# Every engine of a gated-memory kernel in a written order, with eight PSUM banks in turn and TensorE turning part of q and k

## The chip, the cores and the metric

One core of a Trainium2 chip. The metric is the device time of one execution in microseconds (us), of which several are taken; the span given with a profile runs from the first to the last instruction of one profiled execution.

## The reference

Four batches (B), eight heads (H), 768 tokens (S), 40 numbers a head (D), so 320 a token over all heads. First a recurrent attention with exponential gates, then a gated block with a causal convolution of five taps:

```python
def _attn_ref(q, k, v, i_gate, f_gate, o_gate):
    for t in range(S):
        m_new = np.maximum(f_gate[:, :, t] + m, i_gate[:, :, t])
        f_stab = np.exp(f_gate[:, :, t] + m - m_new)
        i_stab = np.exp(i_gate[:, :, t] - m_new)
        C = f_stab[:, :, None, None] * C + i_stab[:, :, None, None] * np.einsum('bhd,bhe->bhde', vt, kt)
        n = f_stab[:, :, None] * n + i_stab[:, :, None] * kt
        denom = np.maximum(np.abs(np.einsum('bhd,bhd->bh', n, qt)), 1.0)
        y[:, :, t] = sigmoid(o_gate) * np.einsum('bhde,bhe->bhd', C, qt) / denom
def _moe_ref(x, w_val, conv_w, w_out):
    gate_pre = sum(conv_w[k] * xp[:, k:k + S, :] for k in range(5))
    return (1.0 / (1.0 + np.exp(-gate_pre)) * (x @ w_val)) @ w_out
```

(`vt`, `kt`, `qt` are token t of v, k and q; `xp` is x with four zero rows ahead.) The second part's x is y with the heads side by side. Its weights arrive as float64 and are turned into float32 on the chip by integer operations (lines 586 to 606).

## The kernel before

The 768 tokens are six tiles j of 128. A tile and a batch b make a unit u, so there are 24; each unit has two chunks of 64 tokens, 48 chunks g in all. The recurrence over time is written per chunk as products of matrices, with the running state C and n carried from a chunk of a batch to the next.

*Preparation, per tile and batch.* q and k are loaded (L188, L192), the largest magnitude is taken on ScalarE (`prep_max`, L288), a power of two as scale comes from it on VectorE (`prep_scale`, L293 to L300), and each number becomes two float16 parts: the high part in `prep_hi` (L324 GpSimd for tile 0, L326 ScalarE for q, L327 VectorE for k of the later tiles), the low one in `prep_lo` (L332 VectorE). They lie in `stk`, tokens on partitions. `prep_tr` (L350) turns a half, q or k of one batch, with a DMA that transposes, issued on SP's queue, into `tq` or `tk`: 48 such transfers. k is also copied into `kp` by DMAs (L197), v and the output gate are loaded (L201, L204).

*Per chunk.* `args` (L360, TensorE) forms sums of gates into `psd`, `expo` (L371, ScalarE) their exponential `dm`. `scores` (L387, TensorE, eight products) gives q times k, `pss`; `probs` (L394, VectorE) multiplies scores by decays into `pt`. `keyw` (L406) weights the keys on GpSimd, `state` (L421, TensorE) makes the next state in `pc`, `state_out` (L434, ScalarE) copies it out. `heads` (L444, TensorE) reads the result out into `ph`.

*Per unit.* `norm` (L459 to L463, VectorE) forms one over the denominator, `norm_o` (L468, GpSimd) multiplies the output gate by it, `gate_o` (L473, VectorE) gives x. `x_tr` (L482) turns x on TensorE in three pieces, `x_copy` (L490 to L492, ScalarE) copies it out of PSUM, once rounded for TensorE and once whole; `x_rest` takes the low part (L498, GpSimd), the piece of 64 channels (L497, VectorE) and the four last tokens of the tile before (L500, L501, GpSimd).

*Per tile, the gated block.* `conv0` (L507, GpSimd) is the first tap, `conv` (L513, VectorE) the others, eight per tile; `conv3` (L525, TensorE) the last 64 channels as ten products; `sigmoid` (L533). `val` (L548, TensorE, three groups of eight products into `pf`), `z_mul` (L553, VectorE), `z_hi` (L557, ScalarE) and `z_lo` (L562, GpSimd) split the product into two parts, `outp` (L574, TensorE, eight products into `po`), `outp_st` (L579, ScalarE) and `out_dma` (L583). The last tile does this in halves of two batches.

*The order.* The start is written out by hand (L692). The rest gets a due time from the table `LAGS`, in units of a chunk; all steps are sorted by it into a program:

```python
    ctx.enter_context(tc.manual_schedule(engines={mybir.EngineType.SP}))
    ps_s = ctx.enter_context(tc.tile_pool(name="ps_s", bufs=NSH, space=PS))
    ps_h = ctx.enter_context(tc.tile_pool(name="ps_h", bufs=2, space=PS))
    ps_c = ctx.enter_context(tc.tile_pool(name="ps_c", bufs=1, space=PS))
    for _, _, fn, a in sorted(work, key=lambda w: w[:2]):
        fn(*a)
```

SP's queue runs in this program order; the other engines get theirs from the framework's scheduler, which starts from it and may move instructions. PSUM has eight banks: five (`ps_s`) serve all short work, two (`ps_h`) `heads`, one (`ps_c`) `state`.

Of the kernel before, what the change touches and what calls it, by code (L numbers as in the profile page):

```python
# [18 lines left out]

LAGS = {  # L20
    "cons1": -5.183, "cons1d": 0, "cons2": 0.457, "cons2d": 2.675, "wgt": 3.44, "wgtd": 0.804, "close": 2.831,
    "og": -7.359, "kp": -5.611, "kpd": 1.009, "vc": -3.927, "vcd": 0.989, "nat": -14.361, "natd": 0.826,
    "sig_o": -3.584, "max": -9.51, "hi": -8.451, "lo": -6.85, "lod": 0.308, "tr": -5.254, "den": -0.323,
    "dend": 0.177, "rs": 1.457, "gate": 3.86, "x_tr": 4.721, "x_copy": 6.057, "x_rest": 7.056, "args": -3.401,
    "expo": -3.399, "scores": -2.076, "probs": -1.445, "keyw": -2.703, "state": -0.531, "state_out": 0.189,
    "heads": -0.632, "conv0": 4.698, "conv0d": 0.9, "conv": 5.393, "convd": 0.299, "sig": 8.436, "val": 8.878,
    "vald": 0.463, "z": 9.375, "zh": 9.181, "zl": 9.511, "outp": 13.042, "outpd": 0.257, "ob": 15.39, "od": 14.45,
    "sig0": -0.329, "maxd": 0.014, "early": 0.441, "conv3": 8.55, "scaled": 0, "e_conv0": 5.797, "e_conv0d": 0.226,
    "e_conv": 4.49, "e_convd": 0, "e_conv3": 3.873, "e_sig": 7.715, "e_val": 6.616, "e_vald": 0.359, "e_z": 8.556,
    "e_zh": 8.123, "e_zl": 8.811, "e_outp": 11.131, "e_outpd": 0.989, "e_ob": 9.909, "e_od": 11.211, "half": 2.582,  # L30
    "si1": 1.548, "og1": 4.264, "sig1": 4.352, "vc1": -3.33, "kpe": 0, "natq": -13.409, "natqd": 0, "qmax": -10.547,
    "qmaxd": 0.075, "qhi": -9.634, "qlo": -8.762, "qtr": -8.036, "qd": 1.073, "qmul": -9.356, "qout": -3.776,
    "kpi": 6.531, "qe1": 0.864, "nat2": 0.089, "og2": -0.141, "sig2": -0.871, "qe2": 0.725, "og3": -0.415,
    "tr3": 0.74, "kp0": -1.411, "si1q": 1, "on_act_hi": 0, "on_act_dup": 0, "on_dve_state": 0, "on_dve_out": 0,
    "on_dve_x": 0, "on_dve_xl": 0, "on_dve_rs": 0, "on_dve_kw": 0, "on_dve_zl": 0, "z@2": 13.103, "zh@2": 13.406,
# [907 lines left out]
```

## Time and profile before

| | |
|---|---|
| median of 3 runs | 287.59 us (287.15 to 287.76) |
| profiled execution, own time | 289.57 us |
| its span | 287.8 us |
| mean granted clock of TensorE | 0.905 |
| busy: TensorE, VectorE, ScalarE, GpSimd | 228.3, 223.5, 172.6, 156.1 us |

The profiled execution is one of its own, 1.98 us over the median. Busy time counts instructions that work; register, branch, semaphore and DMA-issuing ones are left out. PE is TensorE, PEld its loading of weights (which lies beside PE), DVE VectorE, ACT ScalarE, POOL GpSimd and SP SyncE. Matmuls are pipelined and their ends are modelled, so a busy PE is not one at its peak.

### The profile page before, as it was taken

Reading aid. Unit: us, or ns where it says so; the run is one execution under the profiler, and the core shown is the slowest. Engines: PE = TensorE matmul, PEld = TensorE weight load, DVE = VectorE, ACT = ScalarE, POOL = GpSimd, SP = SyncE. Lnnn points to the kernel's source line nnn. Section 1 sums busy time; section 2 is a strip of 40 time slices with the busy share of each in tenths; the row PEclk is TensorE's granted clock in tenths of the full one; section 3 lists DMA queues with packets and bytes.
Section 4 is the critical chain, followed back from the end, with each engine's and each line's share of the span. In section 5 each row is a group of like instructions: output and inputs, shape, how many; then the busy total and the mean of one; then the engine's idle time right before and its main releaser. Section 6 shows DMA issues by size and latency. Waiting matters only on the chain.

```text
span 287.8 us, 6601 instructions
## 1 busy us (share of the span) xinstructions
PE 228.3 (79%) x2411; PEld 186.9 (65%) x2411; DVE 223.5 (78%) x498; ACT 172.6 (60%) x376; POOL 156.1 (54%) x236
## 2 busy tenths in 40 slices
PE   0038827835976876977899999989999999999885
PEld 0027626624865765655698776876678977887874
DVE  7899979746799999877998679997359944973940
ACT  4266555574797774589664596853595466346262
POOL 7694614322878465848935349541369162944451
PEclk9999999575895579999589999996899999999999
DMA  7899899998999996999963899949759640020112
GB/s 139 150 143 176 113 204 142 202 199 135 203 164 224 186 170 62 186 172 208 171 64 59 148 217 208 158 61 167 181 129 128 168 62 3 0 71 24 46 48 92
DMA packets 145897, 38.73 MB, mean 135 GB/s; under 512 B 135176, under 2 KB 143752, under 8 KB 145864
## 3 DMA queue, kind: packets, MB, share of 16 engines
q1 hardware_dynamic: 143044, 37.76, 83.6%
q10 hardware_dynamic: 2820, 0.54, 1.2%
q8 instruction: 19, 0.31, 0.5%
q14 instruction: 14, 0.11, 0.2%
HBM read 17.87 MB, written 4.23 MB: 77 GB/s over the span
## 4 chain that ended last, share of the span: by engine, by line
PE 45%; DMA 16%; DVE 9%; SPq 4%; issue 4%; ACT 3%; POOL 3%; ACTq 0%; DVEq 0%; POOLq 0%
PE ph L444 12%; PE po L574 7%; PE pss L387 6%; DMA tk<-stk 6%; PE pc L421 5%; PE pf L548 5%; PE pg L525 4%; PE psd L360 3%; DMA kp<-nat 3%; PE px L482 3%; DVE sg L513 3%; DMA vc<-in_v_dram 3%; SPq L350 2%; DMA nat<-in_q_dram 2%; DVE pt L394 2%
## 5 line engine op out<-in xcount | busy, mean ns | idle before, releaser
L444 PEld LDWEIGHTS ph<-vc,pt 128*64 128x64 f32 (+1 forms) x768 | 57.6, 159 | 24.4 <-ACT vc L434 12.0
L444 PE MATMUL ph<-vc,pt 128*64 128x41 f32 (+1 forms) x768 | 63.5, 251 | 11.5 <-ACT vc L434 9.1
L406 POOL TENSOR_TENSOR kw<-kp,dm 128x320 f32<-128x320 f32 (+1 forms) x44 | 36.9, 841 | 31.1 <-PE pc L421 12.0
L421 PE MATMUL pc<-vc,kw 128*40 128x41 f32 (+1 forms) x704 | 43.8, 225 | 11.8 <-POOL kw L406 7.3
L513 DVE SCALAR_TENSOR_TENSOR sg<-xc,cwt,sg 128x512 f32<-128x512 f32 (+1 forms) x56 | 48.0, 884 | 3.2 <-POOL sg L507 3.1
L421 PEld LDWEIGHTS pc<-vc,kw 128*40 128x40 f32 (+1 forms) x704 | 37.5, 138 | 18.6 <-issue 9.1
L394 DVE SCALAR_TENSOR_TENSOR pt<-pss,cmp,dm 128x512 f32<-128x512 f32 x48 | 35.5, 741 | 10.1 <-PE pss L387 6.5
L387 PE MATMUL pss<-tq,tk 120*128 120x64 f16 x384 | 33.4, 259 | 8.1 <-DMA tk<-stk 3.4
L360 PE MATMUL psd<-ra,la 120*128 120x512 bf16 x48 | 22.8, 475 | 20.5 <-DMA la<-gda 18.6
L468 POOL TENSOR_TENSOR rs<-sg,den 128x320 f32<-128x320 f32 x24 | 20.5, 854 | 32.1 <-DVE den L463 23.8
L371 ACT ACTIVATE dm<-psd 128x512 f32<-128x512 f32 x48 | 28.4, 596 | 13.6 <-issue 6.5
L387 PEld LDWEIGHTS <-tk 120*128 120x128 f16 x384 | 26.4, 128 | 14.9 <-issue 7.2
L332 DVE SCALAR_TENSOR_TENSOR stk<-nat,scl,stk 128x320 f16<-128x320 f32 x48 | 31.4, 662 | 4.0 <-ACT stk L326 3.3
L288 ACT ACTIVATE junk<-nat 128x320 bf16<-128x320 f32 x48 | 22.5, 469 | 17.0 <-DMA nat<-in_q_dram 7.5
L498 POOL TENSOR_TENSOR xl<-xc,xh 128x256 fp32r<-128x256 f32 x24 | 20.0, 833 | 22.8 <-ACT xc L491 22.8
L434 ACT COPY vc<-pc 40x328 f32<-40x328 f32 x44 | 18.7, 425 | 15.8 <-PE pc L421 14.3
L553 DVE TENSOR_TENSOR sg<-pf,sg 128x512 f32<-128x512 f32 (+3 forms) x21 | 12.6, 610 | 13.5 <-ACT sg L533 6.9
L326 ACT ACTIVATE stk<-nat,scl 128x640 f16<-128x640 f32 x20 | 16.1, 822 | 9.9 <-DMA tq<-stk 7.3
L562 POOL TENSOR_TENSOR zl<-sg,zh 128x512 fp32r<-128x512 f32 (+1 forms) x14 | 15.9, 1139 | 11.0 <-ACT zh L557 10.9
L574 PE MATMUL po<-woh,zh 128*128 128x320 f32 x72 | 20.2, 337 | 0.8 <-POOL zh L562 0.8
L360 PEld LDWEIGHTS <-la 120*128 120x128 bf16 x48 | 5.7, 120 | 20.5 <-issue 19.5
L574 PE MATMUL po<-wol,zh 128*128 128x320 f32 x72 | 18.4, 309 | 0.0
(151 smaller groups left out, 465.9 us busy)
## 6 DMA issues: line engine op xcount, KB each, us to landing
nat<-in_q_dram SPq DMA_DIRECT2D x24, 160.0 KB, 3.4
vc<-in_v_dram SPq DMA_DIRECT2D x12, 320.0 KB, 5.6
sg<-in_o_gate_dram SPq DMA_DIRECT2D x6, 640.0 KB, 7.3
out_dram<-ob SPq DMA_DIRECT2D x24, 160.0 KB, 1.9
kp<-nat SPq DMA_DIRECT2D x22, 160.0 KB, 4.3
nat<-in_k_dram SPq DMA_DIRECT2D x10, 320.0 KB, 4.1
...
```

What stands on the lines that cost most here:

```text
L288: nc.scalar.activation(junk, part(j, x, i), AF.Abs, accum_out=amx[j % 2][:, x, i : i + 1])
L332: return nc.vector.scalar_tensor_tensor(t[:, :, lo : lo + D], part(j, x, i), scl[j % 2][:, x, i : i + 1], t[:, :, 0:D], op0=ALU.mult, op1= ...
L360: nc.tensor.matmul(psd, la[:, p, j, b], ra[:, :, j], start=True, stop=True,)
L371: nc.scalar.activation(dm, psd_[g], AF.Exp)
L387: nc.tensor.matmul(o, tk[h], tq[:, h], start=True, stop=True)
L394: nc.vector.scalar_tensor_tensor(pt, pss_[g], cmp_[j % 2][:, p, b : b + 1], dmt[g], op0=ALU.mult, op1=ALU.mult)
L406: (nc.vector if turn("on_dve_kw", b) else nc.gpsimd).tensor_mul(kw[0:n], kp[0:n, p, b * H : (b + 1) * H], dmt[g][0:n, :, L - 1 : L].to_bro ...
L421: nc.tensor.matmul(pc[n0 : n0 + D, h], kwt[g][0 : ROWS[p], h], vc[j % 2][0 : ROWS[p], p, b * H + h], start=True, stop=True)
L444: nc.tensor.matmul(pht[u][p * L : (p + 1) * L, h], ptt[g][0 : ROWS[p], h], vc[j % 2][0 : ROWS[p], p, b * H + h], start=True, stop=True,)
L468: (nc.vector if turn("on_dve_rs", b) else nc.gpsimd).tensor_mul(rs, og[j % 2][:, b * H : (b + 1) * H], dnt[u].to_broadcast([P, H, D]))
L513: nc.vector.scalar_tensor_tensor(o, xc[j % 2][:, c, b0:b1, t : t + P], cwt[:, c, t : t + 1], o, op0=ALU.mult, op1=ALU.add)
L574: nc.tensor.matmul(pf, z, w, start=(i == 0), stop=(i == len(mm) - 1))
```

## The change

The table of due times and the sort are gone. A string `PLAN` lists every step of the program; a step names its function, its numbers and the engine (`=V` VectorE, `=A` ScalarE, `=P` GpSimd, `=S` SP) or, for TensorE, the PSUM bank (`#0` to `#7`). All engines now run in that written order. The eight banks are one set; any step takes any bank. Buffers are picked by the chunk's or unit's number.

```diff
-    ctx.enter_context(tc.manual_schedule(engines={mybir.EngineType.SP}))
+    ctx.enter_context(tc.manual_schedule())
...
-    ps_s = ctx.enter_context(tc.tile_pool(name="ps_s", bufs=NSH, space=PS))
-    ps_h = ctx.enter_context(tc.tile_pool(name="ps_h", bufs=2, space=PS))
-    ps_c = ctx.enter_context(tc.tile_pool(name="ps_c", bufs=1, space=PS))
+    banks = [psp.tile([P, 512], F32, name=f"bank{i}") for i in range(8)]
...
+ldq.2.3=S wcv.5.7=V laj.1=V args.2#1 trp.0.3.0#3 scs.1.1.2.0.2.1=V lo.0.3.1=V ldk.2.0.2=S expo.0=A wcv.0.0=V ldv.0.1=S
...
+    def trp(b, j, i, x):
+        t = banks[b].bitcast(F16).rearrange("p (h n) -> p h n", h=H)
+        for h in range(H):
+            nc.tensor.transpose(t[0:K3, h], stk[(j * B + i) % NSTK][:, x, h, 0:K3], id16)
+        late["tr", j, i, x] = t
+
+    def trc(e, j, i, x):
+        put[e](turned(j, i, x)[0:K3], late["tr", j, i, x][0:K3])
...
+    for step in PLAN.split():
+        step, _, b_ = step.partition("#")
+        step, _, e = step.partition("=")
+        name, *num = step.split(".")
+        steps[name](int(b_) if b_ else e, *(int(n) if n.isdigit() else n for n in num))
```

What else differs:

- *Turning.* `trp` turns a half of tiles 0 and 1 with eight TensorE transposes into a bank read as float16, `trc` copies it to `tq` or `tk`: 16 halves, 7 copies on VectorE and 9 on ScalarE. `trd` is the DMA for tiles 2 to 5: 32 transfers instead of 48.
- *Engines.* Weighted keys: 24 GpSimd and 20 VectorE (44 GpSimd before). Output-gate product: 17 and 7 (24 and 0). Low part of x: 10 and 14 (24 and 0). Low part of z: 2 and 19 (21 and 0). The low parts of the weights: 7 on VectorE. High parts of q and k: 37 ScalarE, 8 VectorE, 3 GpSimd (20, 20 and 8). Of the copies out of PSUM that ScalarE made, VectorE takes 10 of the state, 6 of the output, 6, 5 and 6 of the three of x; and 6 of the 21 roundings of z. The carried tokens of x go to all three engines (GpSimd before).
- *The spread of the gate sums* (`spread_out`, L258 and L263) is issued on SP's queue, one piece excepted (ScalarE's before).
- *Counts up to `heads` of chunk 23*, before and now: `outp` 3 and 0, `val` 3 and 3 groups, `conv3` 1 and 1, `conv` taps 14 and 8. From there to the last `heads`: `outp` 11 and 13, `val` 9 and 9, `conv3` 3 and 4, taps 24 and 28.

Three places where the order moves. First SP's queue near the start (`nat` are q and k of a tile, `sg` the output gate, `gdg` and `gda` the spread gate sums, which go back into `ra` and `la`; `rawc` are taps). Before:

```order
L188 DMA nat0_81<-in_k_dram 128x8x40
L350 DMA_TRANSPOSE tq0_232<-stk0_114 128x8x128
L350 DMA_TRANSPOSE tk0_100<-stk0_114 128x8x128
L201 DMA vc0_84<-in_v_dram 64x32x40
L270 DMA ra_88<-gdg0_124 24x8x64
L272 DMA la_87<-gda0_126 24x4x64 x2
```

Now, on the same queue:

```order
L414 DMA nat0_78<-in_k_dram 128x8x40
L861 DMA rawc_151<-in_moe_conv_w_dram 128x5x2
L414 DMA nat1_79<-in_k_dram 128x16x40 x2
L426 DMA sg_83<-in_o_gate_dram 128x32x40
L465 DMA gdg0_140<-gsp0_138 32x6x64
L471 DMA gda0_142<-gsp0_138 48x1x64 x3
L423 DMA vc0_81<-in_v_dram 64x32x40
L478 DMA ra_85<-gdg0_140 24x8x64
L482 DMA la_84<-gda0_142 24x4x64 x2
```

The transposing transfers of tile 0 are gone, and the taps, the k of tile 1 and an output gate stand ahead of the gate sums, whose spread is now on this queue.

Second, VectorE around the units between the halves of the program. Before, near the end of tile 2 (`pt` is `probs`, `den` is `norm`, `sg` from `xc` a tap, `sg` from `pf` is `z_mul`):

```order
L553 TENSOR_TENSOR sg_86<-pf0_1_0_1620,sg_86 128x512
L394 SCALAR_TENSOR_TENSOR pt22_1699<-pss22_1650,cmp0_103,dm22_1562 128x512
L553 TENSOR_TENSOR sg_86<-pf0_2_0_1660,sg_86 64x512
L316 COPY sct1_106<-pq3_1673 128x4
L459 TENSOR_SCALAR den10_1724<-ph10_1609,sct0_105 128x8
L513 SCALAR_TENSOR_TENSOR sg_86<-xc1_90,cwt_99,sg_86 128x512
L461 TENSOR_TENSOR den10_1724<-ph10_1609,den10_1724 128x8
L394 SCALAR_TENSOR_TENSOR pt23_1755<-pss23_1714,cmp0_103,dm23_1633 128x512
```

Now, on VectorE in a unit with the same steps (`kw` weighted keys, `rs` the output-gate product, `xl` the low part of x, `vc` from a bank the state's copy):

```order
L704 TENSOR_TENSOR xl0_612<-xc0_86,xh0_610 128x2x128
L635 COPY vc1_82<-bank3_71 40x328
L609 SCALAR_TENSOR_TENSOR pt0_119<-bank7_75,cmp0_102,dm1_117 128x512
L616 TENSOR_TENSOR kw0_121<-kp_80,dm0_116 128x320
L511 TENSOR_SCALAR scl1_110<-amx1_112 128x2
L659 TENSOR_TENSOR rs1_127<-sg_83,den0_123 128x320
L704 TENSOR_TENSOR xl1_613<-xc1_87,xh1_611 128x2x128
L609 SCALAR_TENSOR_TENSOR pt1_120<-bank1_69,cmp0_102,dm2_118 128x512
```

Between two `probs` of VectorE there stand weighted keys, output-gate products and low parts of x, which GpSimd did before, and the state's copy, which ScalarE did.

Third, TensorE after the last `heads`. Before, `outp` of tile 3 is still to come there, then all of tile 4 and tile 5 one after the other:

```order
L574 MATMUL po3_3_3312<-woh_97,zh_592 128x320 x2
L574 MATMUL po3_3_3312<-wol_98,zh_592 128x320 x2
L574 MATMUL po3_3_3312<-woh_97,zl_593 128x320 x2
L574 MATMUL po3_3_3312<-woh_97,zh_592 128x320
L574 MATMUL po3_3_3312<-wol_98,zh_592 128x320
L482 MATMUL px22_3345<-ident_80,x22_3282 128x128 x2
L482 MATMUL px22_3345<-ident_80,x22_3282 64x128
L525 MATMUL pg4_0_3363<-x30_91,cdh_93 64x512 x5
```

Now, on TensorE, the `val` products of tile 5 (L763, 256 columns) have an `outp` of tile 4 (L786) behind each piece:

```order
L763 MATMUL bank7_75<-xh1_611,wvh_92 128x256 x2
L763 MATMUL bank7_75<-xh1_611,wvl_93 128x256 x2
L763 MATMUL bank7_75<-xl1_613,wvh_92 128x256 x2
L763 MATMUL bank7_75<-x31_89,wvh_92 128x256
L763 MATMUL bank7_75<-x31_89,wvl_93 128x256
L786 MATMUL bank0_68<-woh_94,zh_614 128x320 x2
L786 MATMUL bank0_68<-wol_95,zh_614 128x320 x2
L786 MATMUL bank0_68<-woh_94,zl_615 128x320 x2
L786 MATMUL bank0_68<-woh_94,zh_614 128x320
L786 MATMUL bank0_68<-wol_95,zh_614 128x320
```

Pieces of two tiles now alternate in the last part, where before tile 4 was finished first.

## Rows read from the trace of the kernel before

**Rows 1.** The page: span, and busy time of each engine (share, instructions).

```profile
span 287.8 us, 6601 instructions
PE 228.3 (79%) x2411; PEld 186.9 (65%) x2411; DVE 223.5 (78%) x498; ACT 172.6 (60%) x376; POOL 156.1 (54%) x236
```

**Rows 2.** Windows, line 444 alone: stretch, length, busy PE, PEld (instructions), clock, DMA share, GB/s.

```profile
0.00:149.00 149.00, 35.73 (x384) 32.78 (x384) 0.84 1.11 165
```

**Rows 3.** Windows, all lines: stretch, length, busy PE, PEld, DVE, ACT, POOL, the rest as above.

```profile
0.00:149.00 149.00, 97.48 (x1077) 78.94 (x1078) 127.24 (x298) 92.98 (x210) 87.06 (x138) 0.84 1.11 165
...
149.00:253.00 104.00, 101.47 (x1152) 82.01 (x1148) 78.97 (x165) 63.12 (x131) 55.64 (x81) 0.97 0.72 117
253.00:288.00 35.00, 29.31 (x194) 25.96 (x192) 17.31 (x37) 16.45 (x37) 13.35 (x17) 1.00 0.16 58
```

**Rows 4.** VectorE's groups, 0 to 149 us: count, busy us, mean ns, idle before.

```profile
L332 DVE SCALAR_TENSOR_TENSOR stk<-nat,scl,stk 128x320 f16<-128x320 f32 x31 | 21.6, 707 | 2.3 <-ACT stk L326 1.7 <-POOL stk L324 0.6
...
L513 DVE SCALAR_TENSOR_TENSOR sg<-xc,cwt,sg 128x512 f32<-128x512 f32 x14 | 13.8, 1000 | 1.0 <-POOL sg L507 1.0
L327 DVE TENSOR_SCALAR stk<-nat,scl 128x640 f16<-128x640 f32 x12 | 7.8, 648 | 4.3 <-DMA tk<-stk 4.2
```

**Rows 5.** By line, whole kernel: shortest, median and longest in ns; shapes.

```profile
L513 DVE SCALAR_TENSOR_TENSOR sg<-xc,cwt,sg x56: 469/740/1762, 83.7 to 274.0; 128x512 f32<-128x512 f32 x40, 128x256 f32<-128x256 f32 x16
...
L394 DVE SCALAR_TENSOR_TENSOR pt<-pss,cmp,dm x48: 701/740/752, 22.7 to 247.9; 128x512 f32<-128x512 f32 x48
...
L332 DVE SCALAR_TENSOR_TENSOR stk<-nat,scl,stk x48: 493/543/1842, 9.4 to 227.0; 128x320 f16<-128x320 f32 x48
```

**Rows 6.** The chain of waits: start us, length us, what; pieces by DMA.

```profile
42.38 8.73 DMA tk<-stk
...
60.75 3.95 DMA nat<-in_k_dram
...
65.44 3.64 DMA tq<-stk
...
124.37 4.18 DMA kp<-nat
...
132.48 7.23 DMA tk<-stk
```

**Rows 7.** By line, VectorE rows nearest to the operations it gets.

```profile
L473 DVE TENSOR_TENSOR x<-ph,rs x24: 470/479/492, 42.3 to 257.6; 128x320 f32<-128x320 f32 x24
...
L602 DVE SCALAR_TENSOR_TENSOR wo<-ce_o,ca_o x2: 492/1096/1700, 122.4 to 130.3; 128x320 f32<-128x320 f32 x2
...
L786 DVE COPY la<-tl x5: 409/411/414, 36.5 to 38.6; 120x1024 bf16<-120x1024 bf16 x5
...
L553 DVE TENSOR_TENSOR sg<-pf,sg x21: 406/683/692, 128.9 to 279.6; 128x512 f32<-128x512 f32 x10, 64x512 f32<-64x512 f32 x5, 128x256 f32<-128x256 f32 x4, 64x256 f32<-64x256 f32 x2
```

**Rows 8.** GpSimd's groups, 0 to 149 us, columns as in rows 4.

```profile
L406 POOL TENSOR_TENSOR kw<-kp,dm 128x320 f32<-128x320 f32 (+1 forms) x25 | 21.3, 857 | 20.4 <-DMA kp<-nat 7.3 <-PE pc L421 4.3 <-ACT dm L371 2.1
L468 POOL TENSOR_TENSOR rs<-sg,den 128x320 f32<-128x320 f32 x11 | 9.4, 850 | 17.2 <-DVE den L463 9.0 <-DVE scl L295 7.5 <-DVE amx L293 0.7
L324 POOL TENSOR_SCALAR stk<-nat,scl 128x640 f16<-128x640 f32 x8 | 8.9, 1128 | 6.1 <-DVE scl L295 6.1
L498 POOL TENSOR_TENSOR xl<-xc,xh 128x256 fp32r<-128x256 f32 x10 | 8.6, 863 | 1.9 <-ACT xc L491 1.9
```

**Rows 9.** The chain of waits: TensorE pieces (start us, length us, instructions).

```profile
51.16 0.61 PE pss L387 x8
...
151.41 1.22 PE po L574 x8
...
159.27 2.57 PE pg L525 x10
...
216.98 0.48 PE px L482 x3
```

**Rows 10.** TensorE's timeline: its first instruction, and what it waited for.

```profile
18.61 0.58 PE L360 MATMUL psd<-ra,la 120*128 120x512 bf16 x1 [18.61 <-DMA la<-gda]
```

More of the change, by code (lines that the diff above doesn't have):

```diff
@@ L16 @@
 AX = mybir.AxisListType
[L20 to L35, printed above, removed]
[49 rows of a table removed]
-}
@@ L122, in tile_mlstm_gated_ffn @@
     PB = P // B
[L123 removed]
+    K3 = 3 * D
+    MASKE = 0x7F800000
     TOK = (L, 0)
@@ L257, in spread_out @@
-    def spread_out(i, dma):
-        dma(
+    tl = sp.tile([KA, 2, B, P], BF16, name="tl")
+    tr = sp.tile([KA, H, L], BF16, name="tr")
+    sel = sp.tile([P, 2, B], BF16, name="sel")
+    oh1 = sp.tile([P, H], BF16, name="oh")
+    io_ = sp.tile([P, L], F32, name="iota_s")
+    wide = conv_w.dtype != F32
+    WT = I32 if wide else F32
+    raws = [cst.tile([P, DM, 2] if wide else [P, DM], WT, name=f"raw{i}") for i in range(2)]
+    rawc = cst.tile([P, 15, 2] if wide else [P, 15], WT, name="rawc")
@@ new lines, in tile_mlstm_gated_ffn, with bank, fill @@
+    wf = cst.tile([P, DM], F32, name="wf")
+    wa, we, wx = (cst.tile([P, DM], I32, name=n) for n in ("wa", "we", "wx"))
+    ch = cst.tile([P, 2, 5], F32R, name="ch")
+    idm = cst.tile([P, L], F32, name="idm")
+    late = {}
+    def bank(b, *shape):
+        n = 1
+        for s in shape:
+            n *= s
+        t = banks[b][:, 0:n]
+        if len(shape) == 1:
+            return t
+        return t.rearrange("p (a b) -> p a b", a=shape[0])
+    def fill(t, pattern, base, op=ALU.not_equal, v=1.0, m=1):
+        G.affine_select(out=t, in_=t, pattern=pattern, compare_op=op, fill=v, base=base, channel_multiplier=m)
@@ new lines, in zvc, with ovc, zgt, selb @@
+    def zvc(e, i):
+        eng[e].memset(vc[i][0:L, 0], 0.0)
+    def ovc(e, i, p):
+        eng[e].memset(vc[i][TOK[p] : TOK[p] + L, p, :, D:DT], 1.0)
+    def zgt(e):
+        eng[e].memset(gt[L:P, 2], 0.0)
+    def selb(e):
+        with nc.allow_low_precision("one of each sum is 1, the others 0"):
+            V.tensor_reduce(sel_b, ident.rearrange("p (b g) -> p b g", b=B), axis=AX.X, op=ALU.add)
+    def selg(e):
+        V.tensor_reduce(sel_g, ident.rearrange("p (b g) -> p g b", b=B), axis=AX.X, op=ALU.add)
@@ L367, in args @@
-        psd_[g] = psd
-    def expo(g):
-        dm = wk.tile([P, H, L], F32, name=f"dm{g}", tag="dm", bufs=3)
-        nc.scalar.activation(dm, psd_[g], AF.Exp)
-        dmt[g] = dm
-    def scores(g):
-        u, p = divmod(g, 2)
-        j, b = divmod(u, B)
-        k0 = [p * P + h * (P + L) for h in range(H)]
-        tk = [tk_[u % 3][0:K3, c : c + P] for c in k0]
+        return u, p, j, b
+    def args(b_, g):
+        u, p, j, b = ujb(g)
+        psd = bank(b_, H, L)
+        nc.tensor.matmul(psd, la[:, p, j, b], ra[:, :, j], start=True, stop=True)
+        late["psd", g] = psd
@@ L384, in scores @@
-        pss = ps_s.tile([P, H, L], F32, name=f"pss{g}", tag="big")
+            tq = tqs[j % NTQ][0:K3, :, :, c0 : c0 + L // R].rearrange("k r h g -> k h r g")
+        pss = bank(b_, H, L)
         for h in range(H):
@@ L559, in z_lo, with zhi @@
[L559 removed]
+        z = gt[0:n, m, b0:b1]
+        V.tensor_mul(z, late["pf", j, m, b0][0:n], z)
+    def zhi(e, j, m, b0, b1):
         n = P if m < 2 else L
[L561 to L571 removed]
+        put[e](late["zh"][0:n, m, b0:b1], gt[0:n, m, b0:b1])
@@ L816, in tile_mlstm_gated_ffn @@
-    work = []
-    last = (last_pool.ins, last_dve.ins)
-    def at(t, fn, *a):
-        work.append((t, len(work), fn, a))
-    def drain(t0, dt, n, it):
-        def some():
-            with tc.issue_after(last[0]), tc.issue_after(last[1]):
-                for _ in range(n):
-                    next(it, None)
-        for k in range(40):
-            at(t0 + k * dt, some)
-        at(t0 + 40 * dt, run, it)
-    drain(T["cons1"], T["cons1d"], 1, consts1())
-    drain(T["cons2"], T["cons2d"], 1, consts2())
@@ L907, in tile_mlstm_gated_ffn, with obc, od @@
-    for j in range(NJ - 1):
-        feed(j, (j + 1) * SJ, 0, B)
-    for i in range(2):
-        feed(NJ - 1, NG + T["half"] * i, 2 * i, 2 * i + 2, "e_")
-    for _, _, fn, a in sorted(work, key=lambda w: w[:2]):
-        fn(*a)
+            nc.tensor.matmul(po, z, w, start=(i == 0), stop=(i == len(mm) - 1))
+        late["po", j, b] = po
+    def obc(e, j, b):
+        put[e](obs[(j * B + b) % NOB], late["po", j, b])
+    def od(e, j, b):
+        dma(e)(out[b, j * P : (j + 1) * P, :], obs[(j * B + b) % NOB])
```

1100 lines of the change are left out of this document (542 added, 558 removed), and 49 rows, old and new, of the table LAGS.

## The prediction

> **What bounds the kernel now.** I read the totals first, then a table by stretch, then the waits inside the worst stretch. The totals name no single bound: TensorE is busy for 228.3 us and VectorE for 223.5 us of a span of 287.8 us [rows 1]. The table by stretch does. I cut it at 149 us, where TensorE has done 384 of its 768 readout products, that is, heads of chunks 0 to 23 [rows 2], and at 253 us, past the last of them. In the first stretch VectorE works 127.24 of 149 us and TensorE 97.48; in the second TensorE works 101.47 of 104 us and VectorE 78.97; in the last TensorE works 29.31 of 35 us [rows 3]. So VectorE holds the first half, with 21.8 us idle, and TensorE the second, with hardly anything idle. ScalarE (92.98) and GpSimd (87.06) have slack.
>
> Two things inflate the first half. One is stretched VectorE instructions: the mean of the low-part subtraction there is 707 ns and of a conv tap 1000 ns [rows 4], while their medians over the kernel are 543 and 740 ns; the probabilities, whose first input lies in PSUM, run from 701 to 752 ns and never stretch [rows 5]. The other is waits for halves of q and k that a DMA turns: the chain shows 8.73, 3.64 and 7.23 us for three of them, and about 4 us each for a load and a copy of k [rows 6].
>
> **The change, stretch by stretch** (chunks 0 to 23, 24 to 47, and the rest; the counts are those of the order of the instructions before and after).
>
> *First stretch, VectorE.* Onto it come 12 weighted-key products. They read SBUF twice at 128x320; the row of that size is 0.48 us, and the same shape took 1.70 us at worst when another engine was in the way [rows 7]; I take 0.48, 5.8 us in all (up to about 13 at the 1.1 us mean of that group). Six weight subtractions of the same shape: 2.9 us. Seven copies of a turned half (120x1024, out of PSUM): no row shows one. An SBUF copy of 120x1024 took 0.41 us, and a product of 512 columns out of PSUM 0.683, twice which is 1.37 [rows 7]; I take 1.2, nearer the PSUM row, 8.4 us (2.9 to 9.6). Four state copies at 0.48: 1.9. Four copies of pieces of x, no dearer: 1.6. Nine single small products and copies at about 0.5: 4.5 (11 when stretched). Sum: +25. Off it go five scalings of k (5 x 0.65 = 3.2), seven table copies (7 x 0.41 = 2.9), three constant copies (at the same 0.41, 1.2), and six conv taps at 1.0 that now run after chunk 23: -13. Net +12, to 139.
>
> *Stretching.* Mean less median over two groups [rows 4, 5] gives 31 x 0.164 + 14 x 0.260 = 8.7 us, and smaller groups add some. GpSimd's work in the stretch falls from 87 us to under half: of its big groups [rows 8] it keeps 13 of 25 weighted keys, 9 of 11 output-gate products and 3 of 10 low parts of x, and gives up most of the eight scalings. If its work is what stretches VectorE, most of that goes: I take -8, 131 busy. The other end is that none goes.
>
> The Trainium skill (Perfetto Trace Analysis, Optimizing Scalar/DVE Operations) speaks against this edit: where VectorE is saturated it would move work away from it, and it warns that moving work between VectorE and GpSimd may not help because they share a port. That the PSUM-reading row never stretches agrees with a shared port.
>
> *First stretch, waits.* Tiles 0 and 1 no longer wait for DMA turning: 16 steps of eight TensorE transposes each replace 16 of the 48 transfers. Two of the three waits above, 12.4 us, are theirs. The cover that hides the 128 transposes is TensorE's 51 us of idle time. Their price is bounded by three 128x128 turns in 0.48 us and eight 64-column products in 0.61 [rows 9]: 16 x 0.61 = 10 to 128 x 0.16 = 20 us, beside VectorE either way; TensorE's 97.5 becomes about 110. If that cover were gone they would cost their full 10 to 20. What is late next is VectorE itself: I leave it 6 us idle of 21.8 (9.4 if only the 12.4 goes, and less because moved work fills gaps). First stretch: **137 us**; 128 with cheap copies and 3 us more idle gone; 153 if it keeps all 21.8.
>
> The Trainium skill (VectorE: DVE Perf Modes, The three transpose paths) gives 390 ns for a TensorE transpose of 128x128 bf16. By it, as an estimate, the 128 would take 50 us and TensorE about 144 in the first stretch, which could not end under that, and the sum would be 285 or more; the 160 ns measured for a turn of f32 speaks against it, and no row shows a turn of f16.
>
> *The start.* The spread of the gate sums moves from ScalarE's queue to SP's, behind loads that were issued later before. The first decay product waits until 18.61 us for that transfer [rows 10]; behind more bytes it may come at up to 27. I add nothing: VectorE then has some 30 us of preparation ahead of its first probabilities, so this delay costs only what VectorE idles, 0 to 8 us.
>
> *Second stretch.* TensorE does 13 outputs where 11 stood, and four gate products of the third channel where three stood: 2 x 1.22 + 2.57 = +5.0 us [rows 9]; as many products leave the first stretch. VectorE gets 8 weighted keys, 9 low parts of x, 5 output-gate products, 18 copies out of PSUM and 3 of z at 0.48 (20.6 us), 10 low parts of z at 0.68 and 4 conv taps at 1.0: +31; seven scalings of k leave it (7 x 0.65 = 4.5), and of the stretching I take off 4: 79 + 31 - 4.5 - 4 = 101. TensorE stays just the bound: 101.5 + 5.0, its granted clock already 0.97 of the upper level, 2.4 GHz, in the mean [rows 3]. **106 us** (101 if the order packs better, 111 if the two engines wait for each other).
>
> *Last stretch.* Eleven outputs instead of ten, two third-channel products instead of three, as many value products: **35 us** (33 to 37). The pieces of tile 4 stand between those of tile 5 now, which covers waits of VectorE and ScalarE, but TensorE was already busy 29.31 of 35.
>
> **Sum:** 137 + 106 + 35 = 278 us of span, -9.8. The profiled execution took 289.57 us with a span of 287.8; the median of the runs is 287.59, 0.2 under that span. So 277.8 us.
>
> **The rivals.**
> *B, a larger gain.* All stretching goes and the fixed order leaves VectorE no more than 5 us idle in the first half: 128 + 102 + 34 = 264. For it: GpSimd's share falls by half. Against it: an order fixed beforehand must guess every duration.
> *C, the change does not do what it says.* The turned halves come no earlier, because a half now goes ScalarE or VectorE, TensorE, then a copy on an engine that is as full; the wait for the DMA turns into a wait for that copy. Or the turns are dearer than the row: at 0.4 us each the 128 would fill the 51 us that TensorE idles. Either way the first half keeps its length: 149 + 104 + 35 = 288. For it: the chain also holds loads and copies of k of 4 us each [rows 6], which stay. Against the second way stands the 0.16 us of a turn [rows 9]; of C's chance I give it a tenth.
> The figure of the Trainium skill for a turn, given above (VectorE: DVE Perf Modes, The three transpose paths), is C's second way.
> *D, slower.* VectorE saturates. Before, each engine took its instructions in an order that a scheduler chose; now a late input stops all behind it on that engine. VectorE has 131 us of work and keeps the 21.8 us idle: 153. In the second half its 101 us and TensorE's 106 wait on each other: 111, and the end 36: 300. It decides from about 18 us of VectorE idle time in the first half (131 + 18 = 149). For it: VectorE gets 56 us of added work over the two stretches. Against it: a VectorE that idles has a DMA as its last releaser in the dearest rows, and that is what goes.
>
> The advice of the Trainium skill named above (Perfetto Trace Analysis, Optimizing Scalar/DVE Operations) is D's: a full VectorE that is given more. The table by stretch agrees with it on how full VectorE is, and no run here shows the outcome.
>
> **How the numbers follow.** What a measurement of this kernel can tell from no change is about 0.2%, 0.6 us. The forecast (270 to 285) has 0.48, B 0.15, C 0.17 and D 0.20. C lies around zero: 0.06 of it faster, 0.05 within 0.6 us, 0.06 slower. Faster: 0.48 + 0.15 + 0.06 = 0.69; same 0.05; slower 0.06 + 0.20 = 0.26. The range goes from B's 264, leaving out a third to a half of B, to 294, leaving out two thirds of D: 0.19 outside. The likeliest case alone spans 270 to 285.
>
> **What would show it.** Right: heads of chunk 23 end near 137 us; VectorE is busy for over 93% until then; the conv taps' mean falls towards 740 ns; no wait of over 3 us for a turned half in tiles 0 and 1; turning takes 10 to 20 us of TensorE; GpSimd is busy for half its 156 us or less. Wrong: VectorE idles more than 18 us ahead of chunk 23 (D), waits for the copies of turned halves stand in the chain (C), or the second stretch, where TensorE has no slack, takes under 100 or over 111 us.

## The result and the profile after

The change takes the median from 287.37 to 264.4 us (four executions each): a ratio of 0.92, interval 0.9148 to 0.9253, so 23 us less where the forecast had 9.8. The time lies inside the range, near its lower end, at the 264 us of rival B.

The page of the changed kernel, the lines that answer to [rows 1]:

```profile
span 263.7 us, 6791 instructions
PE 222.5 (84%) x2539; PEld 186.9 (71%) x2539; DVE 235.4 (89%) x600; ACT 182.1 (69%) x399; POOL 74.4 (28%) x126
```

GpSimd's work is less than half of what it was, VectorE's is 12 us more. The windows, cut as in [rows 2, 3] (columns as there): first line 643 alone, which is `heads` now, then all lines.

```profile
0.00:127.20 127.20, 29.59 (x384) 26.94 (x384) 0.86 1.09 161
```

```profile
0.00:127.20 127.20, 90.46 (x1208) 75.28 (x1209) 116.40 (x312) 104.54 (x236) 41.30 (x76) 0.86 1.09 161
127.20:231.00 103.80, 103.19 (x1155) 85.38 (x1152) 95.36 (x229) 64.22 (x134) 27.74 (x44) 0.85 0.70 116
231.00:264.00 33.00, 28.81 (x184) 26.27 (x182) 23.63 (x62) 13.30 (x30) 5.38 (x7) 0.83 0.17 61
```

The first stretch gives 21.8 us of the 24 by which the span shrank, the last one 2, the middle nothing in this execution. TensorE's granted clock (as a share of its upper level, 2.4 GHz) was 0.85 in the middle stretch here, against 0.97 before. In a run below that has the same steps there (a_t0_dma) it was 1.00, and the stretch took 3.5 us less, with TensorE busy for 97.51 instead of 103.19:

```profile
137.90:238.20 100.30, 97.51 (x1154) 80.80 (x1152) 94.21 (x228) 64.58 (x136) 27.70 (x45) 1.00 0.67 120
```

So the middle stretch of the changed kernel can be some 3 us shorter than the 104 of before, though not in the execution profiled here. In the first stretch, VectorE is busy for 116.4 us where it was 127.24, and idle for 10.8 where it was 21.8: half the gain is shorter work, half is shorter waiting. TensorE is busy for 90.46 us there instead of 97.48, although 11.8 us of turns were added: the same 384 readout products alone take 29.59 us instead of the 35.73 of [rows 2]. The same three tiles one by one, before and after:

```profile
0.00:58.00 58.00, 28.58 (x325) 23.52 (x326) 50.08 (x126) 29.95 (x64) 31.11 (x56) 0.94 1.04 159
58.00:100.10 42.10, 28.87 (x348) 24.42 (x344) 33.27 (x79) 30.23 (x69) 23.34 (x42) 0.69 1.16 185
100.10:149.20 49.10, 40.24 (x422) 31.20 (x418) 44.07 (x94) 33.00 (x77) 32.62 (x41) 0.85 1.15 154
```

```profile
0.00:64.30 64.30, 33.87 (x464) 29.09 (x465) 57.37 (x161) 50.76 (x103) 19.49 (x43) 0.89 0.91 141
64.30:92.50 28.20, 23.71 (x340) 19.53 (x339) 26.89 (x70) 23.02 (x65) 11.81 (x15) 0.85 1.29 179
92.50:127.20 34.70, 32.88 (x409) 26.66 (x409) 32.14 (x82) 30.76 (x69) 10.00 (x18) 0.82 1.27 184
```

Tile 0 got 6 us longer. TensorE's first instructions, and its first decay product (line 587):

```profile
24.96 1.32 PE L571 MATMUL bank<-idh,stk 128*120 128x128 f16 x10 [24.96 <-DVE stk L554]
```

```profile
30.72 0.85 PE L571 MATMUL bank<-idh,stk 128*120 128x128 f16 x6
31.36 1.06 PE L587 MATMUL bank<-ra,la 120*128 120x512 bf16 x2
```

The first instruction, at 24.96 us (18.61 before [rows 10]), is now a turn, and it waits for a low part that VectorE makes; VectorE is busy for 57.37 us in tile 0, where it was 50.08. Tiles 1 and 2 got 14 us shorter each, and VectorE idles for only 1.3 us in tile 1, where it had 8.8.

VectorE's groups, 0 to 127.2 us after (count, busy us, mean ns, as in [rows 4]):

```profile
L554 DVE SCALAR_TENSOR_TENSOR stk<-nat,scl,stk 128x320 f16<-128x320 f32 x31 | 17.5, 577 | 1.5 <-ACT stk L545 1.3
L721 DVE SCALAR_TENSOR_TENSOR sg<-xc,cwt,sg 128x512 f32<-128x512 f32 x8 | 7.0, 884 | 0.0
L616 DVE TENSOR_TENSOR kw<-kp,dm 104x320 f32<-104x320 f32 (+1 forms) x12 | 5.8, 484 | 0.3 <-PE bank L626 0.3
L547 DVE TENSOR_SCALAR stk<-nat,scl 128x640 f16<-128x640 f32 x7 | 4.0, 566 | 0.3 <-PE bank L571 0.2
L516 DVE TENSOR_SCALAR cmp<-amx 64x2 int32<-64x2 int32 (+1 forms) x18 | 3.9, 214 | 0.4
L511 DVE TENSOR_SCALAR scl<-amx 128x2 int32<-128x2 int32 (+1 forms) x13 | 3.7, 287 | 0.0
...
L575 DVE COPY tk<-bank 120x1024 f16<-120x1024 f16 x4 | 2.6, 682 | 0.4 <-PE bank L571 0.4
...
L509 DVE TENSOR_SCALAR amx<-amx 128x2 int32<-128x2 int32 (+1 forms) x14 | 2.0, 160 | 0.0
...
L507 DVE TENSOR_SCALAR amx<-amx 128x2 f32<-128x2 f32 (+1 forms) x14 | 2.0, 152 | 0.8 <-ACT junk L493 0.8
```

`cmp`, `scl` and the two groups of `amx` are small steps of the scale, mostly of two elements. In the kernel before, over 0 to 149 us, the same four groups read:

```profile
L293 DVE TENSOR_SCALAR amx<-amx 128x2 f32<-128x2 f32 (+1 forms) x15 | 5.4, 362 | 2.4 <-ACT junk L288 2.3
L294 DVE TENSOR_SCALAR amx<-amx 128x2 int32<-128x2 int32 (+1 forms) x14 | 4.9, 352 | 0.2
L300 DVE TENSOR_SCALAR cmp<-amx 64x2 int32<-64x2 int32 (+1 forms) x20 | 3.7, 183 | 0.4
...
L295 DVE TENSOR_SCALAR scl<-amx 128x2 int32<-128x2 int32 (+1 forms) x14 | 2.6, 184 | 0.3
```

A step of 152 ns took 362: the stretching sat in small steps too, not only in the large groups that the prediction counted. But not all small steps got shorter: `scl` went from 184 to 287 ns and `cmp` from 183 to 214, so the four groups together fell by only 5 us, from 16.6 to 11.6. To size the stretching over all groups, I take for each operation and shape the lowest mean that any run of this study shows in any stretch, and count what lies above it. By that measure VectorE's stretch in the first half falls from 30.9 to 12.2 us (the sums of durations are 141.7 and 133.6; instructions overlap at their ends, so these exceed the busy time). How shapes are grouped moves each of the two by about 1 us.

### The profile page after: what moved, and what is told of

It reads as the page before. It is cut to its first block, busy times and chain, and to the rows that moved or that the text cites. A ratio compares the mean times of both kernels' runs of the same rounds, so it can differ in the third digit from the quotient of the medians.

```text
span 263.7 us, 6791 instructions
## 1 busy us (share of the span) xinstructions
PE 222.5 (84%) x2539; PEld 186.9 (71%) x2539; DVE 235.4 (89%) x600; ACT 182.1 (69%) x399; POOL 74.4 (28%) x126
## 4 chain that ended last, share of the span: by engine, by line
PE 50%; DVE 30%; ACT 9%; issue 5%; DMA 3%; SPq 1%; DVEq 0%; ACTq 0%
PE bank L643 11%; PE bank L763 9%; PE bank L786 9%; PE bank L626 6%; PE bank L604 5%; PE bank L742 5%; DVE pt L609 4%; DVE stk L554 4%; DVE sg L721 3%; PE bank L587 3%; DMA tq<-stk 2%; PE bank L674 2%; ACT stk L545 2%; ACT sg L753 2%; DMA nat<-in_k_dram 1%
## 5 line engine op out<-in xcount | busy, mean ns | idle before, releaser
L643 PEld LDWEIGHTS bank<-vc,pt 128*64 128x64 f32 (+1 forms) x768 | 52.5, 148 | 12.9 <-DVE pt L609 7.9
L643 PE MATMUL bank<-vc,pt 128*64 128x41 f32 (+1 forms) x768 | 57.8, 239 | 3.0 <-DVE pt L609 2.9
L591 ACT ACTIVATE dm<-bank 128x512 f32<-128x512 f32 x48 | 28.3, 596 | 15.3 <-PE bank L587 10.3
L609 DVE SCALAR_TENSOR_TENSOR pt<-bank,cmp,dm 128x512 f32<-128x512 f32 x48 | 35.3, 745 | 2.7 <-PE bank L643 1.2
L626 PE MATMUL bank<-vc,kw 128*40 128x41 f32 (+1 forms) x704 | 36.1, 207 | 2.0 <-DVE kw L616 0.8
L626 PEld LDWEIGHTS bank<-vc,kw 128*40 128x40 f32 (+1 forms) x704 | 31.4, 121 | 6.2 <-issue 2.4
L571 PE MATMUL bank<-idh,stk 128*120 128x128 f16 x128 | 11.8, 255 | 27.1 <-DVE stk L554 26.8
L571 PEld LDWEIGHTS <-stk 128*120 128x120 f16 x128 | 10.7, 163 | 28.1 <-DVE stk L554 27.2
L604 PE MATMUL bank<-tq,tk 120*128 120x64 f16 x384 | 28.9, 249 | 1.5 <-DVE wa L824 1.0
L635 ACT COPY vc<-bank 40x328 f32<-40x328 f32 x34 | 14.5, 425 | 13.9 <-PE bank L626 13.2
L587 PE MATMUL bank<-ra,la 120*128 120x512 bf16 x48 | 19.3, 439 | 3.4 <-DVE tq L575 2.7
L786 PE MATMUL bank<-woh,zh 128*128 128x320 f32 x72 | 20.5, 341 | 0.0
L786 PE MATMUL bank<-wol,zh 128*128 128x320 f32 x72 | 19.2, 322 | 0.0
```

Source lines behind the costliest of these rows:

```text
L587: nc.tensor.matmul(psd, la[:, p, j, b], ra[:, :, j], start=True, stop=True)
L591: A.activation(dms[g % NDM], late["psd", g], AF.Exp)
L604: nc.tensor.matmul(o, tk[h], tq[:, h], start=True, stop=True)
L609: V.scalar_tensor_tensor(pts[g % NPT], late["pss", g], cmp_[j % 2][:, p, b : b + 1], dms[g % NDM], op0=ALU.mult, op1=ALU.mult)
L626: nc.tensor.matmul(pc[n0 : n0 + D, h], kws[g % NKW][0:n, h], vc[j % 2][0:n, p, b * H + h], start=True, stop=True)
L643: nc.tensor.matmul(ph[p * L : (p + 1) * L, h], pts[g % NPT][0:n, h], vc[j % 2][0:n, p, b * H + h], start=True, stop=True)
```

## The experiments

Times are medians; ratios are to the kernel before. Where a trace is read, "first half" ends with `heads` of chunk 23.

### Turning by DMA again

```diff
-trp.0.0.0#0 trc.0.0.0=V
+trd.0.0.0=S
```

and so for all 16 halves (a_dma_turn), for tile 1 alone (a_t1_dma), for tile 0 alone (a_t0_dma).

> The changed kernel with the halves of q and k of tiles 0 and 1 turned by DMA again (48 such transfers, no TensorE turns, no copies). Theory W (the gain is the waits for turned halves): the 12.4 us of waits come back, the first stretch (heads of chunks 0 to 23) ends at about 139 us instead of 127, 276 us in all. Theory P (GpSimd stretched VectorE, and its work is gone) and theory O (the written order): VectorE is rid of 7 copies (4.6 us), the stretch moves by under 4 us, 260 to 268 us.

> The changed kernel with tile 1 turned by DMA, tile 0 still by TensorE, so that the start is the same. With both tiles by DMA tile 1 took 37.6 us against 28.2. Theory W: tile 1 alone costs those 9 us again, 272 to 276 us. Rival (the loss came from the late start of tile 0): 264 to 267 us.

> The changed kernel with tile 0 turned by DMA, tile 1 by TensorE. With both by DMA the time was 286.7 us, with tile 1 alone 278.0. If the two add up: 264.4 + 8.7 = 273 us, with the first decay product at about 34 us, since the spread of the gate sums stands behind transfers that wait for VectorE. If the loss of both was tile 1's alone: 266 us.

| turned by DMA | us | ratio, interval |
|---|---|---|
| none (the change) | 264.4 | 0.92, 0.9148 to 0.9253 |
| tile 0 | 271.8 | 0.9413, 0.9331 to 0.9495 |
| tile 1 | 278.0 | 0.9623, 0.9551 to 0.9695 |
| both | 286.7 | 0.9947, 0.99 to 0.9994 |

The two add up: 7.4 + 13.6 = 21.0 us against 22.3 for both. So in the new order nearly the whole gain hangs on the turning, and theory W holds there, with a larger sum than its 12 us. The transfers stand where the turns stood, and the order was not written anew around them; what the best order with DMA turns would take is not shown. Tile 0's part is the start. TensorE's waits with both tiles by DMA:

```profile
PE bank L585 <- DMA la<-gda: 33.9, 1, 33.9
PE bank L602 <- DMA tk<-stk: 15.3, 2, 10.8
```

(Columns: total us, times, longest.) The transfers that turn wait for VectorE on SP's queue, and the spread of the gate sums stands behind them; the first decay product waits to 33.9 us, against 31.4 with the turns on TensorE, and then up to 10.8 us for a turned k. Tile 1's part is seen in the waits of ScalarE, VectorE and SP's queue (from 60, 60 and 55 us to 112) with tile 1 by DMA:

```profile
ACT stk L543 <- DMA tk<-stk: 7.9, 1, 7.9
```

```profile
DVE stk L552 <- ACT stk L543: 7.4, 2, 6.6
```

```profile
SPq L564 <- DVE stk L552: 8.3, 2, 5.1
```

The two staging buffers `stk` stay taken until the DMA has turned them, so ScalarE cannot write the next high part, VectorE waits for that, and SP's queue (line 564 is the transposing transfer) waits for VectorE: a ring of three queues, each waiting for the next. With TensorE the buffer is free as soon as eight transposes have read it: in the changed kernel ScalarE waits for them once, for 2.2 us.

### Turning on TensorE in the kernel before

```diff
+        if j < 2:
+            for h in range(H):
+                nc.tensor.transpose(tp[0 : 3 * D, h], stk[i % 2][:, x, h, 0 : 3 * D], id16)
+            (nc.vector.tensor_copy if (i + x) % 2 else nc.scalar.copy)(t[0 : 3 * D], tp[0 : 3 * D])
+            return
```

for both tiles (b_pe_turn), and with `j == 1` for tile 1 alone (b_t1_pe).

> The kernel before with the other part alone: halves of tiles 0 and 1 turned by eight TensorE transposes and copied by ScalarE and VectorE in turn, everything else and the scheduler as before. Theory W (the turning is the gain by itself): the waits for turned halves of tiles 0 and 1 go, 12 us or more of the first two tiles (100 us before), 270 to 280 us. Theory V (turning gains only where the order is made for it): the copies and turns wait in the scheduler's order, 284 to 296 us.

> The kernel before with tile 1 alone turned by TensorE, where the scheduler has the order; tile 0, whose order is written by hand, by DMA as before. In the changed kernel tile 1 by DMA cost 13.6 us. Theory W (the turning gains under any order): the 8.7 and 3.6 us waits in tiles 0 and 1 go, 275 to 282 us. Theory V (only under the new order): 286 to 294 us.

Both tiles: 297.1 us, ratio 1.0331 (1.0266 to 1.0395), slower. The start there is written by hand, and TensorE stood behind halves that were not ready:

```profile
PE tp L354 <- DVE stk L333: 33.1, 5, 11.2
```

Tile 1 alone, under the scheduler: 288.2 us, ratio 0.9997 (0.9948 to 1.0046), nothing. The first half is 147.4 us, nearly 2 us shorter than before, and the second 1 us longer. Theory W falls here: the same turning that is worth 13.6 us in the changed kernel is worth nothing in the one before. The order is not the only difference between the two. Here the turned halves also take one of the five banks for short work, which another run below shows to be scarce in this kernel; the two were not told apart.

### The order

```diff
-    ctx.enter_context(tc.manual_schedule())
+    ctx.enter_context(tc.manual_schedule(engines={mybir.EngineType.SP}))
```

with the engines of the table added to the set; the rest go by the scheduler. Steps, engines and banks are those of the change.

> The changed kernel with the same steps on the same engines and banks, but only SP in written order, the other engines ordered by the framework's scheduler as before. Theory O: the written order is what gains; 275 us or more. Theories P and W: the gain goes with the engines, not the order; 262 to 270 us.

> The changed kernel with only SP and TensorE in written order, VectorE, ScalarE and GpSimd ordered by the scheduler (309 us with SP alone written). If the 45 us of the scheduler's order lie on TensorE: 264 to 275 us. If on VectorE: 295 us or more, since TensorE in its fixed order then waits for VectorE.

> The changed kernel with only SP and VectorE in written order. If the scheduler's order of VectorE costs the 45 us: 264 to 275 us. If TensorE's: 295 us or more.

> The changed kernel with only SP and ScalarE in written order. SP alone: 309 us; SP, TensorE and VectorE: 294; with ScalarE to these: 269. If ScalarE's order carries its 25 us by itself: 280 to 287 us. If no engine's order helps unless the others keep it: 300 us or more.

> The changed kernel with SP, TensorE and VectorE in written order, ScalarE and GpSimd by the scheduler. These two have slack, so by theory the order of the full engines is enough: 264 to 272 us. Rival: a late ScalarE (state copies, exponentials) holds both, 280 us or more.

> The changed kernel with SP, TensorE, VectorE and ScalarE in written order, only GpSimd by the scheduler (with ScalarE by the scheduler too it took 294 us). If ScalarE's order holds the 30 us: 264 to 268 us. If GpSimd's: 290 us or more.

| in written order, beside SP | us | ratio, interval |
|---|---|---|
| none (a_sched) | 309.1 | 1.0744, 1.0648 to 1.084 |
| TensorE (a_ord_pe) | 304.4 | 1.0577, 1.0487 to 1.0666 |
| ScalarE (a_ord_act) | 296.0 | 1.0269, 1.0199 to 1.0338 |
| VectorE (a_ord_dve) | 295.0 | 1.0238, 1.0153 to 1.0323 |
| TensorE, VectorE (a_ord_pedve) | 294.3 | 1.0208, 1.011 to 1.0307 |
| those and ScalarE (a_ord_nopool) | 268.9 | 0.9337, 0.9281 to 0.9392 |
| all (the change) | 264.4 | 0.92, 0.9148 to 0.9253 |

The new steps in the scheduler's order are 22 us slower than the kernel before. Windows of a_sched, first half and second:

```profile
0.00:149.20 149.20, 102.08 (x1200) 84.46 (x1201) 124.69 (x335) 110.87 (x244) 49.21 (x81) 0.85 0.90 141
149.20:276.60 127.40, 116.25 (x1185) 93.83 (x1182) 93.27 (x217) 67.02 (x136) 28.58 (x40) 0.89 0.53 92
```

The first half is as long as before the change, although VectorE's stretch there is 13.4 us against 30.9; the second is 23 us longer. Neither of the two full engines in written order brings the time back, nor both: with them fixed, ScalarE's order is worth 25.4 us, though ScalarE is busy for only 104.5 of 127.2 us. The expectation that slack in ScalarE makes its order cheap was wrong. That ScalarE's order alone gives 13 us and on top of the others 25 says that the order works as a whole. Two things were not tried: due times for the scheduler that are fitted to the new steps, as those of `LAGS` were to the old ones, and a written order for the old steps alone. Which instruction of ScalarE comes too late in the scheduler's order was not taken further.

### Work between GpSimd and VectorE

```diff
-keyw.2=V rsm.2=V xlo.1=V zlo.0.0.0.4=V
+keyw.2=P rsm.2=P xlo.1=P zlo.0.0.0.4=P
```

(a_pool_back; these and all others of the four names that were on VectorE.) For b_moved, in the kernel before:

```diff
-    "on_dve_x": 0, "on_dve_xl": 0, "on_dve_rs": 0, "on_dve_kw": 0, "on_dve_zl": 0, "z@2": 13.103, "zh@2": 13.406,
+    "on_dve_x": 0, "on_dve_xl": 2, "on_dve_rs": 1, "on_dve_kw": 2, "on_dve_zl": 4, "z@2": 13.103, "zh@2": 13.406,
```

> The changed kernel with the weighted keys, the output-gate products and the low parts of x and z on GpSimd again, each at its place in the order. Theory P: VectorE's instructions stretch again, by some 10 us or more in the first stretch against 7.6 now, although VectorE has 15 instructions less there (7 us); 268 to 280 us. Rival (a full VectorE is relieved): VectorE's work falls by 7 us in the first stretch and the time with it, 257 to 264 us.

> The kernel before with one part of the change alone: half of the weighted keys and of the low parts of x, a quarter of the output-gate products and all low parts of z on VectorE, in the scheduler's order. Theory P: the stretch of VectorE in the first half falls from 26 us to under 15 and pays for the work that it gets (about 10 us); 278 to 286 us. Theories W and O: VectorE was full and gets more; 290 to 300 us.

Back on GpSimd: 265.8 us, ratio 0.9213 (0.9121 to 0.9304), and its interval overlaps that of the change. Theory P expected a loss; the time lies between the two expectations, at the change's own. The first half:

```profile
0.00:127.80 127.80, 89.29 (x1199) 74.59 (x1200) 113.23 (x295) 104.05 (x234) 51.20 (x90) 0.93 1.06 160
```

VectorE is rid of 15 instructions there and works 3 us less, GpSimd 10 us more, and the half is as long. In the second half VectorE's stretch goes from 7.7 to 18.1 us by the measure above, so that of some 32 instructions less only 4 us of busy time remain (95.4 to 91.1). So no gain of this part by itself is shown. What it can be worth at most is some 3 us: with it taken back the second half took 103.6 us at a granted clock of 1.00, against the 100.3 of a_t0_dma at the same clock. In the kernel before, the move alone costs 2.5% (296.0 us, ratio 1.0255, 1.0144 to 1.0367): the first half ends at 143.9 us, 5 us earlier, and the second takes 114.1 instead of 104. So there the move pays in the half where VectorE is the bound and costs more in the one where TensorE is. Why it costs 10 us there, with VectorE busy for 87 of the 114 us, was not traced.

### GpSimd work that nobody needs

```diff
+    def pj(e):
+        G.tensor_mul(dj, dj, dj)
```

called twice behind each `probs` (a_pool_extra: 96 products of 128x320); for a_pool_memset a fill of the same tile in its place, four behind each `probs`.

> The changed kernel with two idle products more on GpSimd per chunk (128x320, SBUF in and out, used by nothing), 96 in all, about 36 us of GpSimd work in the first stretch. Theory P: VectorE's stretch in the first half goes from 10 us to about 20 and the first half takes 5 to 10 us more; 270 to 280 us. If the stretch is not GpSimd's doing, or VectorE's time doesn't set the end: 264 to 267 us.

> The changed kernel with four fills (128x320, written, nothing read) more on GpSimd per chunk, 192 in all, used by nothing. With two products per chunk that read SBUF the time was 289.6 us and VectorE's work in the first half grew by 14 us. If only GpSimd's reading is in VectorE's way: no growth, 264 to 267 us. If any GpSimd work is: growth in proportion to its time, 275 us or more.

Products: 289.6 us, ratio 1.0046 (0.9997 to 1.0095): the whole gain gone, without one instruction added on VectorE. Fills: 271.8 us, 0.941 (0.933 to 0.949). First halves, products and then fills:

```profile
0.00:140.20 140.20, 93.81 (x1199) 78.59 (x1200) 130.08 (x310) 104.79 (x234) 83.28 (x123) 0.89 0.97 149
```

```profile
0.00:128.90 128.90, 87.80 (x1202) 72.75 (x1203) 119.62 (x310) 104.20 (x234) 76.68 (x172) 0.97 1.07 160
```

The second halves, in the same order:

```profile
140.20:255.20 115.00, 104.99 (x1158) 86.07 (x1156) 107.81 (x228) 64.72 (x137) 69.61 (x94) 0.96 0.60 102
```

```profile
128.90:235.30 106.40, 99.62 (x1155) 81.80 (x1152) 97.91 (x228) 64.59 (x136) 62.17 (x141) 1.00 0.64 112
```

42 us more of products on GpSimd make VectorE's same work 13.7 us longer and the half 13.0 us; 35 us more of fills make it 3.2 and 1.7 us longer. The second half with fills is 2.6 us longer than in the changed kernel's profile, and 6 us longer than in a_t0_dma, which had the same granted clock of 1.00 there. VectorE's weighted keys and taps with products, then with fills:

```profile
L627 DVE TENSOR_TENSOR kw<-kp,dm 104x320 f32<-104x320 f32 (+1 forms) x12 | 8.1, 674 | 0.0
...
L732 DVE SCALAR_TENSOR_TENSOR sg<-xc,cwt,sg 128x512 f32<-128x512 f32 x8 | 7.6, 966 | 1.2 <-POOL sg L726 1.1
```

```profile
L736 DVE SCALAR_TENSOR_TENSOR sg<-xc,cwt,sg 128x512 f32<-128x512 f32 x8 | 5.8, 739 | 0.5 <-POOL sg L730 0.5
...
L631 DVE TENSOR_TENSOR kw<-kp,dm 104x320 f32<-104x320 f32 (+1 forms) x12 | 5.8, 481 | 0.4 <-PE bank L641 0.3
```

GpSimd's reading is what stretches these two groups, 674 and 966 ns against 481 and 739. The Trainium skill (SBUF — State Buffer, SBUF: two separate sides) says that a VectorE operation with two SBUF inputs is kept out by a GpSimd operation only where that one reads SBUF; the two runs agree for these two groups. Reading is not the whole of it: the small steps of the scale grow from 11.6 us to 14.5 with products and to 14.0 with fills, so that most of what fills add to VectorE lies in them; why was not found. In the second half the products cost at least 11 us more (115.0 us): VectorE, with 107.8 us of work, is then busier than TensorE (105.0), so its slack in that half is small. That the added products also delay GpSimd's own work is part of this time: TensorE waits for its weighted keys for 3.1 us.

### Three tries for more

```diff
-trd.2.0.0=S
+trp.2.0.0#1 trc.2.0.0=A
```

and so for the four halves of q of tile 2 (a_t2q_pe). For a_start, eight gate steps of tiles 1 to 5 (`gates.1.2` to `gates.1.9`) stand behind the fourth turn, and two copies of the identity into `kp` and five table copies go to GpSimd. For b_pc2, in the kernel before, `NSH = 4` and two banks for `ps_c`.

> The changed kernel with the four halves of q of tile 2 turned by TensorE too, copies by ScalarE and VectorE in turn, 28 transfers left. Tile 1 turned by DMA cost 13.6 us. Theory W: the 5.5 us wait for a turned half of q at 64 us goes, 258 to 262 us. Theory V (VectorE's total sets the first half): two copies more on VectorE and two on ScalarE, 264 to 267 us.

> The changed kernel with a lighter start of VectorE: the gate steps of tiles 1 to 5 behind the first turns instead of ahead of them, and seven copies of constants on GpSimd. If VectorE's preparation sets the first turn (25 us) and that the end: TensorE starts 4 to 6 us earlier, 259 to 263 us. If only VectorE's total counts: 262 to 265 us. If the gate sums of tile 1 come late: 265 to 270 us.

> The kernel before with two PSUM banks for the state and four instead of five for the short work. If the one bank of the state held VectorE and TensorE back: 282 to 285 us. If the split of the banks is no bound under the scheduler's order: 286 to 290 us.

More turning: 264.9 us, ratio 0.9191 (0.913 to 0.9252), the same as the change. The 5.5 us wait that was to go is gone from the chain, and heads of chunk 23 still end at 127.9 us: it was not a wait that set the end. Lighter start: 267.4 us, 0.9269 (0.9203 to 0.9335), 3 us behind the change. The time lies where late gate sums were to put it, but they are not the reason. In the profiled execution (271.3 us) the first turn came only 1.2 us earlier, at 23.8 us, and what came late was the next turn. The eight gate steps, now in a row, keep VectorE from 26.0 to 36.2 us; TensorE waits 10.7 us for the low part behind them, and its first decay product starts at 39.1 us. Another split of the banks in the kernel before: 299.2 us, 1.0339 (1.0202 to 1.0476). One bank less for short work, and one more for the state, cost 3.4% there, so the banks for short work are a bound in that kernel. In the change's written order up to three banks hold states at a time, up to three hold readouts and up to eight short work, with eight in all, so the old split cannot carry it; what shared banks are worth in the new order was not tried for that reason. No kernel beat the change.

## Why the prediction was wrong

- **The bound was read rightly.** The gain lies in the first stretch; the second stayed at 104 us with TensorE busy for 103.2 (forecast 106), the last took 33 (35). The added 5.0 us of TensorE work in the second stretch do not show: at a granted clock of 1.00 TensorE does it in 97.5 us, less than the 101.5 of before at 0.97. Nor do the turns make TensorE's first stretch 110 us of work; it is 90.5.
- **The step that failed is the size of the stretching**: "most of that goes: I take -8, 131 busy". It went down by 18.7 us, not 8. I had sized it from two groups (8.7 us). By the same mean less median these two now show 2.2 us, so they gave 6.5; the rest lies in groups that I left out. Over all groups it was 30.9 us: in the small steps of the scale, in the gate steps (one of 32x640 fell from 1733 to 584 ns) and in the conversion of the weights as well. That is 10.7 us of the 14.6 by which VectorE's busy time was missed. The other 4 are 1.4 us of moved work and instructions that overlap more (the sums of durations exceed the busy time by 14.5 us before and by 17.2 now). The range of the term ended at 8.7 us; the other rows of the same view would have carried it further.
- **The signs of it** came out in part. The taps' mean fell from 1000 to 884 ns, not to 740, and VectorE was busy for 91.5% of the first stretch, not over 93%. That GpSimd's products stretch VectorE is shown by adding some. The written order is not what took the stretch away: without it (a_sched) it is 13.4 us, nearly as low as the change's 12.2. How much of the 18.7 us came from GpSimd's reads alone is not shown, since the small steps grow with fills too.
- **The net work moved was right**: sums of durations less the stretch are 110.8 and 121.4 us, +10.6 against +12. In it the copies of turned halves, taken at 1.2 us, take 0.68 (3.8 us less for seven), and other steps a little more.
- **VectorE's idle time** was taken at 6 us and is 10.8; with the work 14.6 lower this gives 127.2 instead of 137.
- **The waits** for turned halves of tiles 0 and 1 are gone, and the 128 turns take 11.8 us of TensorE (10 to 20 forecast). What I did not see is that the gain of this hangs on the rest of the change: 21 us with it, none or a loss without.
- **The start**: the first decay product came at 31.4 us against at most 27, and not for the reason given. It does not wait for the transfer of the gate sums; it stands behind the first turns in the written order, and these wait for VectorE. Tile 0 is 6 us longer, against nothing in the sum, and the later tiles make up for it.
- **Rivals.** B's sum (264) was met, at a chance of 0.15, in part by luck. Its first stretch of 128 does not follow from its own words: 139 less all of the 8.7 us plus 5 of idle time is 135. And its mechanism came out only half: 12.2 us of stretch remain and VectorE idles for 10.8 us, not 5. What I held against B, that a fixed order must guess every duration, did not cost what I feared: ordered by the scheduler the same steps take 309 us. C and D are out: no copy of a turned half holds TensorE for over 2.7 us, and VectorE idles less than before. The advice of the Trainium skill to move work off a full VectorE (Perfetto Trace Analysis, Optimizing Scalar/DVE Operations) did not decide: with less work on GpSimd to stretch it, the fuller VectorE was done sooner, and moving four kinds of products back changed the time by no more than its interval, as its warning about the two engines has it.
- **As a whole** I priced the parts and added them. The parts tried alone in the kernel before bring nothing or cost 2.5 to 3.4%; without the written order the rest costs 7%; together they gain 8%. A sum of parts cannot show that.
